# Weights' bound from TensorE products of their upper halves, without identity products, and one more unit with one exponential

## The chip, the cores and the metric

The kernel runs on one core of a Trainium2 chip. The metric is the device time of one execution in microseconds (us). The engines are TensorE (PE in the profile; its weight loads are PEld), VectorE (DVE), ScalarE (ACT), GpSimd (POOL), and SyncE (SP), which issues the transfers. A later kernel is compared with the kernel before by the medians of their runs.

## The reference

A linear attention with random features feeds a two-layer network with GELU. Batch 8, 8 heads, 576 tokens, head size 64, 128 features; the network has model size 512, hidden size 2048, on 8 x 576 = 4608 tokens.

```python
def phi(x):                                  # x: q or k, scaled by D ** -0.25
    proj = np.einsum('bhsd,md->bhsm', x, omega)
    sq = np.sum(x * x, axis=-1, keepdims=True) / 2.0
    h = proj - sq
    h = h - np.max(h, axis=-1, keepdims=True)
    return np.exp(h) / np.sqrt(m)
q_p, k_p = phi(q_s), phi(k_s)
kv = np.einsum('bhsm,bhsd->bhmd', k_p, v)
z = np.sum(k_p, axis=2)
num = np.einsum('bhsm,bhmd->bhsd', q_p, kv)
den = np.einsum('bhsm,bhm->bhs', q_p, z)[..., None] + 1e-06
x = (num / den), heads side by side           # 4608 x 512
h = x @ w_in
g = 0.5 * h * (1.0 + erf(h / sqrt(2)))
out = g @ w_out
```

The two weights come as 64-bit words (the bits of float64) and are made into 32-bit floats on the chip.

## The kernel before, in words

**Attention.** The 64 heads are worked in 32 units of two heads (`units`, four to a batch entry, numbered 0 to 31). Units 0 to 7 are plain, in 32-bit floats (`unit_plain`). A plain unit loads k and q (`load_two`) and v (`load_vraw` with a copy `v_copy` on POOL, or `load_v`), projects both on PE in three steps (`pair`, `shared`, `pair`; lines 657 and 664), takes the maximum of each row on DVE (`top`, line 669), and forms the exponentials of 18 tiles of 128 x 128. In mode 0 (units below `X['m0']`) each tile has an exponential of its own on ACT, with the maximum as bias (`exp_tiles`, line 673). In mode 1 DVE subtracts the maxima in five instructions (`shift_tiles`, line 678) and ACT takes one exponential of the whole unit (`exps`, line 682). Then come k times v on PE (`kv`, line 689), the transposes of q (`q_trans`, `q_copy`, lines 727 and 731), and for each half of the tokens numerator and denominator (`num_plain`, line 737), the reciprocal (`rcp`) and the division (`div`). Units 8 to 31 are split: they work with pairs of high and low parts on all engines.

**Network.** The tokens are cut into 13 blocks: 128 tokens, eleven times 384, then 256. Block 0 is computed with 32-bit products (`mm1` line 1176, `mm2` line 1202) and needs the first 128 tokens, so units 0 to 3. The other blocks use pairs of 16-bit parts, with three products for each (`mm1` line 1181, `mm2` lines 1205 to 1207), and scales that are powers of two.

**Weights.** Each weight comes in eight pieces of 1024 words a partition, w_in first, through two `raw` buffers (`weights_in`). A piece has two transfers of 512 KB (`w_load`), ACT converts the upper words (`w_hi`, line 426) and the lower ones (`w_lo`, line 435), DVE takes the absolute maximum of the raw upper words (`w_rmax`, line 438) and shifts (`w_shift`, line 442), and POOL adds the two (`w_round`, line 453). When the eight maxima of a weight are there, a chain finds the largest of all: `wchain_a` on DVE over the pieces, `wchain_b` a transpose on PE, `wchain_c` on DVE (line 506), `wchain_d` on PE, then the exponent is cut out and the scales are made (`wchain_e`, `wchain_f`). With them each weight is split into two 16-bit parts (`w_high` on ACT, `w_low` on DVE).

**PSUM.** Of the eight banks three go by the name `at`, three by `acc`, two by `h`. The plain units of the first batch entry use all three names for some tiles.

**Order.** Every step is an operation with an engine, a cost and what it reads and writes. They are numbered as they are created. A planner goes through a modelled time and emits for each engine, among the operations that are ready, the one with the earliest due time; due times come from the numbers `STARTS`, `UDUE` and `OFF` and from those in `X`. The operations in `FIRST` are taken in the order of that list, ahead of all others. The order so found is fixed on each engine. Numbers 0 to 5 are constants and omega, 6 to 39 unit 0, 40 to 73 unit 1, 74 to 107 unit 2, 108 to 141 unit 3, 142 to 145 the v of units 4 and 5, 146 to 149 the scale chain of the first batch entry, 151 to 246 the pieces of w_in and then w_out, six operations to a piece, 248 to 253 the scale chain of w_in, 254 to 285 its split. Block 0 has 292 to 373 (292 is its first product), block 1 begins at 421, unit 4 at 582, unit 5 at 614.

**Identity products.** When the planner finds PE free between 5 (`wk0`) and 100 us (`wk`) of its modelled time with nothing to emit, it puts in four products of a 128 x 128 matrix made of bits of the identity (`fill`, line 381), whose result nobody reads. At the very start stand 22 products of zeros (`warm`, line 377).

## Time and profile before

| what | value |
|---|---|
| median of 3 runs | 976.95 us (976.17 to 978.94) |
| the profiled execution | 975.53 us |
| its span, first to last instruction | 973.8 us |
| PE busy | 963.4 us, 99% |
| DVE, ACT, POOL busy | 715.4, 730.0, 350.4 us |
| identity products, line 381 | 312, 21.8 us |

The profile is one execution. A group of instructions reads: line, engine, operation, tile written <- tiles read, shapes, count | busy us, mean ns of one | idle time of its engine just before, and what ended it. A stretch reads: from:to, length, then for each engine busy us and number of instructions, the granted clock of PE, the share of the DMA engines and GB/s. A line of the timeline reads: start us, us, engine, line, operation, tiles, shapes, count [idle time before it <- what ended it]. A line of the waits reads: engine and line <- what it waited for: us in total, times, longest.

### The profile page before, as it was taken

What the parts mean: (1) busy time and instruction counts of PE and PEld (TensorE: products, weight loads), DVE (VectorE), ACT (ScalarE), POOL (GpSimd) and SP (SyncE); (2) the same over time, 40 slices, a digit from 0 to 9 for tenths busy, and PEclk for the clock granted to TensorE, in tenths of its full rate; (3) what the DMA queues carried; (4) which work ended last, traced back from release to release, by engine and by line L of the source; (5) the groups of instructions that cost most, each with busy time, mean ns of one, the idle gap of its engine ahead of it and who ended that gap; (6) DMA issues with size and microseconds to landing.
All of it is one profiled execution on the core that took longest, in us unless ns stands there. A gap on an engine that the chain in (4) does not pass through costs nothing.

```text
span 973.8 us, 18152 instructions
## 1 busy us (share of the span) xinstructions
PE 963.4 (99%) x6324; PEld 602.3 (62%) x6324; DVE 715.4 (73%) x1948; ACT 730.0 (75%) x1504; POOL 350.4 (36%) x560
## 2 busy tenths in 40 slices
PE   8999999999999999999999999999999999999998
PEld 7777665665566666666565665566656656555576
DVE  5899899977888889878797888777767778621111
ACT  6979897887689879787798878877776986643243
POOL 2444334742166264353255335245216522200000
PEclk9999999999999999999999999999999999999999
DMA  8756123321041041031221132022003200000000
GB/s 305 229 182 227 70 73 134 98 82 55 1 118 61 26 139 47 25 91 45 75 82 49 30 127 66 14 72 61 24 33 86 62 23 12 1 33 1 1 34 22
DMA packets 39083, 70.96 MB, mean 73 GB/s; under 512 B 5712, under 2 KB 14288, under 8 KB 38992
## 3 DMA queue, kind: packets, MB, share of 16 engines
q1 hardware_dynamic: 38992, 69.81, 23.1%
q8 instruction: 50, 0.82, 0.4%
q14 instruction: 41, 0.34, 0.1%
HBM read 60.36 MB, written 9.44 MB: 72 GB/s over the span
## 4 chain that ended last, share of the span: by engine, by line
PE 96%; DVE 2%; DMA 1%; ACT 0%; issue 0%; SPq 0%; ACTq 0%; DVEq 0%
PE hb L1181 37%; PE acc L1205 12%; PE acc L1207 12%; PE acc L1206 12%; PE at L746 4%; PE at L924 3%; PE at L902 3%; PE at L1003 2%; PE hb L381 2%; PE hb L1176 2%; PE acc L1202 1%; PE at L657 1%; PE at L737 1%; PE at L689 1%; PE hb L689 1%; PE at L727 1%
## 5 line engine op out<-in xcount | busy, mean ns | idle before, releaser
L1181 PE MATMUL hb<-xh,wih 128*128 128x384 f16 (+1 forms) x768 | 247.2, 322 | 0.6 <-DVE gl L1197 0.4
L1181 PE MATMUL hb<-xl,wih 128*128 128x384 f16 (+1 forms) x768 | 247.2, 322 | 0.0
L1181 PE MATMUL hb<-xh,wil 128*128 128x384 f16 (+1 forms) x768 | 247.1, 322 | 0.0
L894 POOL TENSOR_TENSOR r<-xt,r 64x256 fp32r<-64x256 f32 (+2 forms) x216 | 171.8, 814 | 202.7 <-ACT r L889 161.3
L1205 PE MATMUL acc<-woh,gh 128*128 128x512 f16 (+1 forms) x560 | 211.4, 377 | 0.0
L1207 PE MATMUL acc<-wol,gh 128*128 128x512 f16 (+1 forms) x560 | 210.5, 376 | 0.0
L1206 PE MATMUL acc<-woh,gl 128*128 128x512 f16 (+1 forms) x560 | 210.5, 376 | 0.0
L1197 DVE SCALAR_TENSOR_TENSOR gl<-hb,bs,gh 128x384 f16<-128x384 f32 (+1 forms) x192 | 115.2, 600 | 126.0 <-ACT gh L1193 124.2
L1181 PEld LDWEIGHTS <-wih 128*128 128x128 f16 x1536 | 147.0, 98 | 95.2 <-issue 1.7
L1189 ACT ACTIVATE hb<-hb,bs 128x384 f32<-128x384 f32 (+1 forms) x192 | 104.5, 545 | 86.8 <-PE hb L1181 84.5
L1193 ACT ACTIVATE gh<-hb,bs 128x384 f16<-128x384 f32 (+1 forms) x192 | 109.2, 569 | 51.5 <-PE acc L1207 35.5
L1181 PEld LDWEIGHTS <-wil 128*128 128x128 f16 x768 | 75.1, 98 | 50.2 <-issue 1.6
L889 ACT CAST r<-xt 128x256 fp32r<-128x256 f32 (+2 forms) x216 | 81.5, 403 | 25.8 <-PE at L902 10.5
L1207 PEld LDWEIGHTS <-gh 128*128 128x128 f16 x576 | 56.4, 98 | 64.5
L1205 PEld LDWEIGHTS <-gh 128*128 128x128 f16 x576 | 56.1, 97 | 47.4 <-issue 0.4
L1206 PEld LDWEIGHTS <-gl 128*128 128x128 f16 x576 | 56.5, 98 | 42.1
L803 DVE TENSOR_TENSOR w<-at,rt 64x128 f32<-64x128 f32 (+6 forms) x168 | 54.7, 325 | 4.3 <-DVE rt L770 0.5
L757 ACT ACTIVATE dt<-at,vsc 64x288 f32<-64x288 f32 x96 | 47.6, 495 | 5.2 <-PE at L746 3.0
L902 PE MATMUL at<-om,r 128*128 128x256 f32 x216 | 50.3, 325 | 0.2
L924 PE MATMUL at<-r,om 128*128 128x288 f32 x192 | 50.4, 351 | 0.0
L906 ACT COPY lo<-at 128x256 f32<-128x256 f32 (+1 forms) x120 | 40.4, 349 | 2.2 <-PE at L902 1.5
L963 DVE TENSOR_TENSOR ql<-qt,qh 128x576 fp32r<-128x576 f32 x48 | 37.3, 782 | 6.1 <-ACT qh L960 6.0
(218 smaller groups left out, 1690.6 us busy)
## 6 DMA issues: line engine op xcount, KB each, us to landing
xt<-in_kT SPq DMA_DIRECT2D x56, 288.0 KB, 3.8
xt<-in_qT SPq DMA_DIRECT2D x56, 288.0 KB, 3.6
out_x<-o SPq DMA_DIRECT2D x35, 256.0 KB, 2.1
raw<-in_w_in SPq DMA_DIRECT2D x16, 512.0 KB, 5.2
raw<-in_w_out SPq DMA_DIRECT2D x16, 512.0 KB, 4.6
w<-in_v SPq DMA_DIRECT2D x6, 1280.0 KB, 6.1
wol<-in_v SPq DMA_DIRECT2D x6, 320.0 KB, 5.9
vt<-in_v SPq DMA_DIRECT2D x2, 320.0 KB, 4.1
```

The source lines that it names most:

```text
L803: nc.vector.tensor_tensor(x[r, c0:c1], ps[r, r0:r1], rt[r, r0:r1], op=ALU.mult)
L889: nc.scalar.copy(G['r', u, x][:, 0:b - a], xf[:, a:b])
L894: nc.gpsimd.tensor_tensor(r, xf[D:, a:b], r, op=ALU.subtract)
L902: nc.tensor.matmul(o[:, t], r[:, t * P:(t + 1) * P], om, start=True, stop=True)
L924: nc.tensor.matmul(G['pp', u, NK + g][:, 0:HS], om[:, i], xr_part(u, NK + g), start=(i == 0), stop=(i == 1))
L1181: nc.tensor.matmul(h[:, 0:t], w, (G['xh', n, j], G['xh', n, j], G['xl', n, j])[k][:, 0:t], start=(i == 0), stop=(i == 3 * NJ - 1))
L1189: nc.scalar.activation(h, h, AF.Gelu, scale=G['bs', n][:, 2:3])
L1193: nc.scalar.activation(G['gh', n, c][:, 0:t], G['h', n, c][:, 0:t], AF.Copy, scale=G['bs', n][:, 3:4])
L1197: nc.vector.scalar_tensor_tensor(G['gl', n, c][:, 0:t], G['h', n, c][:, 0:t], G['bs', n][:, 3:4], G['gh', n, c][:, 0:t], op0=ALU.mult, op1 ...
L1205: nc.tensor.matmul(acc, gh[:, s], woh[:, c, c0:c1], start=(c == 0), stop=False)
L1206: nc.tensor.matmul(acc, gl[:, s], woh[:, c, c0:c1], start=False, stop=False)
L1207: nc.tensor.matmul(acc, gh[:, s], wol[:, c, c0:c1], start=False, stop=(c == NF - 1))
```

## The change

- The maximum over the raw upper words (`w_rmax`) is not taken any more. In its place PE multiplies the upper halves (as bf16) of the rounded words with themselves: `w_gram`, eight products of 128 x 128 a piece, summed over four pieces (`GP`) in one PSUM bank. DVE then takes the maximum of that 128 x 128 sum (`w_gmax`). Its diagonal holds sums of squares, so its root bounds the weights; `wchain_e` and `wchain_f` halve the exponent accordingly. A piece still has six operations, with one more for every fourth.
- `wk` goes from 100 to 0: no identity products are put in. (`fill` itself is written a little differently and not called.)
- `m0` goes from 5 to 4: unit 4 takes mode 1 instead of mode 0. `shift_tiles` writes the unit's own tile.
- All numbers of the planner are others, and `FIRST` has 984 entries instead of 752. In it block 0's first product has the number 296, w_in's pieces are 151 to 200, w_out's 201 to 250, the chain of w_in 252 to 257, unit 4 begins at 586, unit 5 at 619.

The diff; of the lists only `FIRST` is shown, up to the entry of block 0's first product:

```diff
--- before.py
+++ after.py
-X = dict(fb=793.51, fbp=-272.45, fb0=327.13, fbb=-89.81, fbw=0.0, pm=0.088, tsw=1.28, wmaxp=0, plain=8, kvp=8, eb0=8, ttr=1,
-         pair=0, amax=0, qm=1, xm=0, km=0, prelu=1, vs=1, rm=1, wk=100.0, wk0=5.0, nd=1, sr=0, pmx=0, m0=5)
...
-FIRST = (1, 3, 0, 2, 6, 7, 8, 40, 4, 5, 42, 110, 76, 144, 41, 142, 10, 9, 151, 157, 44, 13, 43, 11, 14, 15, 47, 74, 16, 45, 17,
-         12, 49, 46, 18, 108, 50, 48, 23, 75, 21, 51, 19, 22, 52, 153, 152, 77, 57, 154, 24, 109, 155, 25, 55, 20, 156, 53,
-         158, 58, 28, 159, 78, 160, 111, 163, 26, 30, 29, 161, 32, 54, 27, 79, 83, 162, 81, 31, 582, 84, 33, 59, 56, 60, 34,
-         61, 85, 169, 112, 80, 35, 164, 165, 62, 66, 166, 167, 36, 63, 168, 115, 67, 82, 37, 113, 171, 170, 86, 114, 175, 38,
-         64, 583, 116, 173, 117, 39, 65, 614, 91, 118, 172, 89, 87, 119, 174, 90, 68, 92, 176, 177, 120, 93, 143, 88, 181, 69,
-         615, 178, 123, 584, 121, 124, 70, 96, 179, 122, 100, 98, 585, 180, 97, 94, 587, 71, 99, 183, 101, 182, 102, 95, 187,
-         72, 588, 125, 185, 586, 73, 184, 103, 130, 145, 589, 131, 126, 134, 186, 132, 647, 104, 135, 127, 133, 590, 128, 105,
-         188, 189, 136, 591, 129, 193, 106, 190, 592, 146, 191, 147, 648, 192, 595, 148, 107, 596, 593, 597, 137, 594, 199,
-         195, 194, 602, 649, 138, 196, 604, 248, 598, 139, 605, 197, 603, 149, 599, 198, 249, 616, 140, 200, 292, 250, 141,
...
+X = dict(fb=647.7, fbp=-229.23, fb0=655.22, fbb=-508.62, fbw=0.0, pm=0.056, tsw=1.28, wmaxp=0, plain=8, kvp=8, eb0=8, ttr=1,
+         pair=0, amax=0, qm=1, xm=0, km=0, prelu=1, vs=1, rm=1, wk=0.0, wk0=5.0, nd=1, sr=0, pmx=0, m0=4, gm=1, rawn=2)
...
+FIRST = (1, 3, 6, 0, 2, 40, 41, 7, 151, 4, 5, 157, 8, 42, 10, 142, 144, 44, 110, 13, 76, 11, 14, 15, 47, 49, 74, 16, 108, 50,
+         45, 12, 17, 152, 18, 158, 154, 75, 9, 21, 46, 19, 43, 23, 48, 160, 51, 20, 57, 24, 22, 77, 153, 28, 58, 111, 78, 159,
+         155, 32, 29, 30, 79, 33, 83, 25, 81, 31, 52, 80, 26, 586, 84, 161, 163, 34, 85, 55, 109, 82, 53, 156, 35, 56, 86, 27,
+         169, 36, 54, 162, 587, 89, 37, 59, 87, 90, 60, 62, 38, 61, 164, 91, 39, 63, 166, 88, 66, 64, 92, 143, 67, 165, 96, 98,
+         97, 167, 100, 65, 101, 99, 112, 170, 68, 115, 171, 176, 113, 117, 172, 116, 168, 619, 118, 173, 69, 114, 119, 70, 588,
+         93, 94, 182, 71, 95, 589, 177, 591, 174, 125, 590, 178, 592, 179, 175, 180, 593, 72, 120, 652, 594, 183, 126, 102,
+         620, 123, 145, 184, 188, 121, 185, 124, 595, 186, 73, 122, 181, 103, 596, 127, 128, 104, 130, 129, 194, 187, 599, 131,
+         134, 132, 653, 597, 189, 105, 600, 598, 133, 135, 191, 190, 136, 146, 106, 601, 192, 147, 107, 137, 195, 607, 201,
+         138, 193, 196, 197, 609, 611, 139, 608, 198, 612, 610, 602, 148, 140, 149, 141, 207, 199, 603, 202, 621, 654, 200,
+         252, 203, 253, 204, 296, 297, 624, 298, 604, 300, 205, 299, 254, 301, 622, 302, 255, 625, 303, 623, 304, 208, 305,
...
@@ -270,6 +281,7 @@
     T0 = [sum(TB[:n]) for n in range(NBLK + 1)]
     assert T0[-1] == NTOK
     NF = F // P
+    GP = 4
     R2 = 2 * S
     NT = R2 // P
     NV = v.shape[3]
@@ -323,7 +335,7 @@
     op = PL.op
     mp, dp, late, G = [], [], [], {}
     bufs = dict(at=3, h=2, acc=3, nm=2, cm=2, ct=2, cg=2, zr=2, km=2, kvz=1, qh=1, kvz2=1, qh2=1, dt=1, rt=1, rc=2, mx=1, nq=1, mc=1, kvs=1,
-                vsc=2, bs=4, be=2, xs=4, raw=2, r=2 if X['xm'] else 3, lo=2, qt=2, ql=2 if X['qm'] else 4, kvh=1, kvl=1, xh=8, xl=8, g=3, gh=3, gl=3, o=2)
+                vsc=2, bs=4, be=2, xs=4, raw=X['rawn'], r=2 if X['xm'] else 3, lo=2, qt=2, ql=2 if X['qm'] else 4, kvh=1, kvl=1, xh=8, xl=8, g=3, gh=3, gl=3, o=2)
     for k, b in bufs.items():
         PL.ring(k, b)
     QW = 2 if X['qm'] else 1
@@ -378,7 +390,7 @@
 
     def fill():
         for i in range(4):
-            nc.tensor.matmul(hb[0][:, T:], iz[:, 0:P], iz[:, P:], start=True, stop=True)
+            nc.tensor.matmul(hb[0][:, T:], iz[:, 0:P], iz[:, P:], start=False, stop=True, skip_group_check=True)
 
     def load_om():
         for r in range(2):
@@ -437,6 +449,15 @@
     def w_rmax(pc):
         nc.vector.tensor_reduce(wmax[:, pc.win, pc.i:pc.i + 1], raw(pc)[2].bitcast(F32), axis=AX.X, op=ALU.max, apply_absolute_value=True)
 
+    def w_gram(pc):
+        o = G['gram', pc.win, pc.i // GP][:, 0:P]
+        for x in range(8):
+            a = pc.b.bitcast(BF16).rearrange("p (x m t) -> p x m t", x=8, t=2)[:, x, :, 1]
+            nc.tensor.matmul(o, a, a, start=(pc.i % GP == 0 and x == 0), stop=(pc.i % GP == GP - 1 and x == 7))
+
+    def w_gmax(win, g):
+        nc.vector.tensor_reduce(wmax[:, win, g:g + 1], G['gram', win, g][:, 0:P], axis=AX.X, op=ALU.max)
+
     def w_shift(pc):
         if X['rm']:
             nc.vector.tensor_scalar(pc.b, pc.b, 3, None, op0=ALU.logical_shift_left)
@@ -494,6 +515,9 @@
         return w32f[:, 0, c], woh[:, c], wol[:, c]
 
     def wchain_a(win):
+        if X['gm']:
+            nc.vector.tensor_reduce(wcm[:, win:win + 1], wmax[:, win, 0:NF // 2 // GP], axis=AX.X, op=ALU.max)
+            return
         w = [i for i in range(NF // 2) if i % 2 == 0 or not X['pmx'] >> (i // 2 + 4 * (1 - win)) & 1]
         st = 2 if len(w) == NF // 4 else 1
         assert st == 2 or len(w) == NF // 2
@@ -509,12 +533,14 @@
         nc.tensor.matmul(G['wps', win][:, P:P + 1], ones, G['wct', win][0:1, 0:1], start=True, stop=True)
 
     def wchain_e(win):
-        nc.vector.tensor_scalar(wsc[:, win, 0:1].bitcast(I32), G['wps', win][:, P:P + 1].bitcast(I32), 0x7ff00000 if X['rm'] else 0x7f800000, None, op0=ALU.bitwise_and)
+        nc.vector.tensor_scalar(wsc[:, win, 0:1].bitcast(I32), G['wps', win][:, P:P + 1].bitcast(I32), 0x7f000000 if X['gm'] else 0x7ff00000 if X['rm'] else 0x7f800000, None, op0=ALU.bitwise_and)
 
     def wchain_f(win):
         e, s, r = (wsc[:, win, i:i + 1].bitcast(I32) for i in range(3))
         one = float(1 << 23)
-        if X['rm']:
+        if X['gm']:
+            nc.gpsimd.tensor_scalar(e, e, 0.5, 65 * one, op0=ALU.mult, op1=ALU.add)
+        elif X['rm']:
             nc.gpsimd.tensor_scalar(e, e, 1.0, -896 * one / 8, op0=ALU.mult, op1=ALU.add)
             nc.gpsimd.tensor_scalar(e, e, 187 * one / 8, 87 * one / 8, op0=ALU.min, op1=ALU.max)
             nc.gpsimd.tensor_scalar(s, e, -8.0, (254 + TOP) * one, op0=ALU.mult, op1=ALU.add)
@@ -544,7 +570,7 @@
         rk, bk = ('raw', win, i), [('w32', win, c) for c in pc.c]
         wl[0] = op('SP', 0.94, w_load, pc, new=[('raw', rk)], size=735e3, after=wl[0])
         op('ACT', 1.08, w_hi, pc, r=[rk], w=bk if X['rm'] else [rk + ('hi',)])
-        if X['rm']:
+        if X['rm'] and not X['gm']:
             op('DVE', 1.23, w_rmax, pc, r=[rk], w=[('wmax', win, i)])
         op('ACT', 1.08, w_lo, pc, r=[rk], w=pc.lk if pc.l is not None else [rk + ('lo',)])
         if not X['sr']:
@@ -559,6 +585,12 @@
         op('POOL', 2.4 + 0.4 * X['sr'], w_round, pc, r=[rk, rk + ('lo',)] + (pc.lk if pc.l is not None else []), w=bk)
         if X['sr'] and not X['prelu']:
             op('DVE', 1.21, w_sign, pc, r=[rk], w=bk)
+        if X['gm']:
+            g = ('gram', win, i // GP)
+            op('PE', 0.46, w_gram, pc, r=bk, w=[g] if i % GP else [], new=[] if i % GP else [(ANY[:2], g)])
+            if i % GP == GP - 1:
+                op('DVE', 0.25, w_gmax, win, i // GP, r=[g], w=[('wmax', win, i // GP)])
+            return
         if X['rm']:
             return
         if X['pmx'] >> (i // 2 + 4 * (1 - win)) & 1:
@@ -675,7 +707,7 @@
     def shift_tiles(u, k, ts):
         n = len(range(2 * NT)[ts])
         pv = G[k][:, 0:n * P].rearrange("p (t m) -> p t m", m=M)
-        nc.vector.tensor_tensor(et[:, ts], pv, G['nm', u][:, ts].unsqueeze(2).broadcast_to([P, n, M]), op=ALU.add)
+        nc.vector.tensor_tensor(u.et[:, ts], pv, G['nm', u][:, ts].unsqueeze(2).broadcast_to([P, n, M]), op=ALU.add)
 
     def exps(*us):
         for u in us:
```

More of the change, by code (lines that the diff above doesn't have):

```diff
@@ L26 @@
 TBS = (128,) + (384,) * 11 + (256,)
-X = dict(fb=793.51, fbp=-272.45, fb0=327.13, fbb=-89.81, fbw=0.0, pm=0.088, tsw=1.28, wmaxp=0, plain=8, kvp=8, eb0=8, ttr=1,
-         pair=0, amax=0, qm=1, xm=0, km=0, prelu=1, vs=1, rm=1, wk=100.0, wk0=5.0, nd=1, sr=0, pmx=0, m0=5)
-STARTS = (526.64, 413.1, 498.14, -519.29, 750.73, 290.96, 409.8, 1471.02, 410.3, 561.38, 1804.53, 1092.9, 2449.47, 1437.07)
-UDUE = (138.05, 1052.37, 451.76, -315.56, -8.29, -412.87, -648.85, -667.31, -702.59, -616.51, 659.91, -322.47, 26.1, 555.78,
[4 rows of a table removed]
@@ L51 @@
-FIRST = (1, 3, 0, 2, 6, 7, 8, 40, 4, 5, 42, 110, 76, 144, 41, 142, 10, 9, 151, 157, 44, 13, 43, 11, 14, 15, 47, 74, 16, 45, 17,
[31 rows of a table removed]
+X = dict(fb=647.7, fbp=-229.23, fb0=655.22, fbb=-508.62, fbw=0.0, pm=0.056, tsw=1.28, wmaxp=0, plain=8, kvp=8, eb0=8, ttr=1,
+         pair=0, amax=0, qm=1, xm=0, km=0, prelu=1, vs=1, rm=1, wk=0.0, wk0=5.0, nd=1, sr=0, pmx=0, m0=4, gm=1, rawn=2)
+STARTS = (412.42, 653.5, 441.15, -677.42, 743.14, 400.93, 780.18, 825.26, 441.66, 285.14, 1439.49, 1000.86, 1810.77, 1167.1)
@@ new lines @@
+UDUE = (176.77, 1015.59, 463.19, -234.55, 109.96, -452.15, -855.33, -883.87, -808.78, -588.47, 512.64, -629.9, -195.61, 817.08,
[4 rows of a table added]
+OFF = dict(block_be=0.84, block_high=-2.56, block_low=0.9, block_out=-1.79, block_spread=10.38, bound_a=162.44, bound_b=14.89,
+           chain_a=64.97, chain_b=-25.49, chain_c=7.47, chain_d=-64.81, den=-73.77, div=132.1, exp_tiles=-0.29, exps=-29.94,
+           g_high=9.53, gelu=17.68, k_low=35.67, k_shift=0.47, kv=10.92, kv_a=0.51, kv_b=42.42, kv_b2=3.03, kv_c=48.29,
+           kv_d=3.07, kv_split=31.59, kvz_plain=-6.79, load_dup=26.25, load_om=-6.31, load_two=-7.52, load_v=29.83,
+           load_vraw=-33.05, load_vst=-4.66, mm1=-64.6, mm2=-18.41, nothing=111.04, num=-106.7, num_plain=-95.35, p2=-3.6,
+           pair=-18.86, proj=26.72, proj_add=13.93, proj_lo=0.73, proj_q=40.57, q_back=23.41, q_blocks=-0.43, q_copy=10.83,
+           q_high=62.65, q_low=-58.16, q_max=50.95, q_max2=25.79, q_max3=3.98, q_max4=-14.62, q_max5=44.93, q_max6=2.41,
+           q_shift=125.5, q_trans=13.48, scale_om=0.18, shared=-33.97, shift_tiles=33.5, split_om=-1.75, store=-0.29,
+           store_dma=97.81, top=1.3, v_a=62.18, v_b=-12.99, v_copy=-2.44, v_max=127.3, v_scales=-6.73, v_spread=11.66,
+           w_gmax=-126.84, w_gram=38.4, w_hi=-0.45, w_high=9.25, w_lo=-0.61, w_low=0.47, w_shift=26.8, warm=2.44,
+           wchain_a=-0.4, wchain_b=3.35, wchain_c=15.67, wchain_e=-21.18, wchain_f=-4.54, x_high=20.23, x_low=-8.93,
+           zeros=-15.48)
```

12 lines of the change are left out of this document (removed), and 64 rows, old and new, of tables (FIRST, UDUE).

## The prediction

> **What bounds the kernel now.** The page comes first: the share of each engine, the slices, and the chain that ended last.
>
> ```profile
> span 973.8 us, 18152 instructions
> ...
> PE 963.4 (99%) x6324; PEld 602.3 (62%) x6324; DVE 715.4 (73%) x1948; ACT 730.0 (75%) x1504; POOL 350.4 (36%) x560
> ...
> DVE  5899899977888889878797888777767778621111
> ACT  6979897887689879787798878877776986643243
> ...
> PE 96%; DVE 2%; DMA 1%; ACT 0%; issue 0%; SPq 0%; ACTq 0%; DVEq 0%
> ```
>
> TensorE (PE) is busy for 99% of the span and owns the chain; VectorE (DVE) and ScalarE (ACT) come to nine tenths only in the first slices. So the time is: when useful work on PE becomes dense, plus all that PE has left to do from there. A busy PE need not be a useful one, since the identity products count too. The second view is therefore the busy time by stretches, of all instructions and then of the identity products (line 381) and of the start-up products (line 377) alone.
>
> ```profile
> core 0: us, PE busy (x) PEld busy (x) DVE busy (x) ACT busy (x) POOL busy (x), PEclk, DMA share, GB/s
> 0.00:10.00 10.00, 6.99 (x62) 5.34 (x64) 2.75 (x14) 2.42 (x5) 1.94 (x8) 1.00 0.68 229
> 10.00:30.00 20.00, 18.90 (x244) 16.40 (x240) 12.62 (x28) 16.82 (x49) 7.06 (x7) 1.00 0.96 316
> 30.00:65.00 35.00, 34.48 (x396) 27.80 (x395) 31.53 (x80) 30.84 (x78) 15.50 (x10) 1.00 0.71 222
> 65.00:112.00 47.00, 45.98 (x364) 34.85 (x364) 43.31 (x86) 40.99 (x61) 19.64 (x20) 1.00 0.49 169
> 112.00:157.00 45.00, 45.00 (x286) 26.17 (x285) 41.59 (x108) 37.45 (x77) 19.08 (x29) 1.00 0.24 64
> 157.00:200.00 43.00, 42.91 (x262) 26.08 (x261) 38.60 (x113) 34.82 (x72) 22.52 (x35) 1.00 0.35 113
> ```
>
> ```profile
> 0.00:10.00 10.00, 0.40 (x4) 0.23 (x4) 1.00 0.68 229
> 10.00:30.00 20.00, 6.75 (x100) 5.84 (x100) 1.00 0.96 316
> 30.00:65.00 35.00, 10.59 (x152) 9.21 (x152) 1.00 0.71 222
> 65.00:112.00 47.00, 4.06 (x56) 3.60 (x56) 1.00 0.49 169
> ```
>
> ```profile
> 0.00:10.00 10.00, 4.23 (x22) 2.93 (x22) 1.00 0.68 229
> ```
>
> Before 65 us PE is busy for 60.4 us, but 17.7 of these are identity products and 4.2 start-up products: 38.4 us are useful. From 65 to 112 us only 4.06 are identity products and 1.02 idle; from 112 us on nothing is spare. The first product of block 0 (line 1176) starts at 64.8 us:
>
> ```profile
> L1176 PE MATMUL hb<-xa,w x128: 272/275/377, 64.8 to 107.9; 128*128 128x128 f32 x128
> ```
>
> So there are two stages. Up to 65 us units 0 to 3 go through DVE and ACT (31.5 and 30.8 of the 35 us from 30 to 65), and PE waits for them. From 65 us on PE sets the end. What the change is worth is the lead L by which block 0 starts earlier, plus what leaves PE's own queue after that, less what is put there.
>
> **The change, part by part.**
>
> *Maxima out, and what the order puts ahead of block 0.* The rows that price it (line 438 is the maximum over raw weights, 682 the one exponential of a unit; the last row is the sum of line 673, the exponentials of single tiles, over the first 200 us):
>
> ```profile
> L438 DVE TENSOR_REDUCE wmax<-raw 128x1 f32<-128x1024 f32 x16 | 19.3, 1207 | 1.0 <-DMA raw<-in_w_in 1.0
> L678 DVE TENSOR_TENSOR et<-at,nm 128x512 f32<-128x512 f32 (+1 forms) x10 | 5.9, 622 | 0.0
> L442 DVE TENSOR_SCALAR w<-w 128x1024 int32<-128x1024 int32 x16 | 10.8, 677 | 0.0
> L506 DVE TENSOR_REDUCE ct<-at 1x1 f32<-1x128 f32 x2 | 0.5, 254 | 0.0
> L435 ACT ACTIVATE w<-raw 128x1024 int32<-128x1024 uint32 x12 | 14.2, 1185 | 0.0
> L731 ACT COPY qh<-at 128x512 f32<-128x512 f32 (+1 forms) x11 | 5.4, 518 | 0.0
> L682 ACT ACTIVATE et<-et x16: 2122/2124/2129, 81.6 to 826.3; 128x2304 f32<-128x2304 f32 x16
> ```
>
> ```profile
> sum 200.00, ACT 26.54; mean ACT 4.42
> ```
>
> Five units of 18 tiles make 90, so a tile's exponential is 0.295 us. In the order written out by hand, block 0's first product is number 292 at place 230 of the old list and 296 at place 238 of the new one. I count what stands ahead of it in each. On DVE eight maxima go (8 x 1.207 = 9.7 us); two small maxima over PSUM come (0.25 each, by the 128-element reduce of line 506), five shift instructions of unit 4 (5.9 / 10 x 5 = 2.95), one weight shift (0.68) and one division (taken as a shift's 0.59): DVE is 4.9 us lighter. On ACT unit 4's 18 tiles go (5.3); one exponential (2.12), one weight conversion (1.19) and one copy (0.49) come: 1.5 us lighter. Over the whole kernel DVE gets 19.3 - 1.0 - 2.95 = 15.3 us lighter and ACT 3.2; but after 65 us both run beside a full PE, and what they save there buys nothing.
>
> L is 1.5 us if ACT sets the stage and 4.9 if DVE does. From 30 to 65 us they are busy for 30.84 and 31.53 us, too close to choose, so I take the middle: L = 3.2 us.
>
> *Identity products out.* Before 65 us they stand where PE waits anyway: 0. After 65 us they and the idle time make 4.06 + 1.02 = 5.1 us that useful work can take: -5.1. New idle time there is taken as 0, because the next stretch, which has no identity product, shows 45.00 busy of 45.00; were it not so, as much of the 5.1 would stay idle, so the other end is 0.
>
> *Products of the weights in.* Each of 16 pieces brings eight products of 128 columns. The nearest row is 52 identity products, of that type and shape, in one run:
>
> ```profile
> 8.66 0.37 PE L657 MATMUL at<-om,xt 64*128 64x128 f32 x1 [1.96 <-DMA xt<-in_kT]
> ...
> 10.34 3.08 PE L381 MATMUL hb<-ident 128*128 128x128 bf16 x52
> ```
>
> That is 59 ns each and 0.47 us a piece. Eight pieces lie ahead of block 0, in PE's idle time; eight after it, on the path: +3.8 us. They read every second half word, so the far end is the 4-byte product of line 1176, at most its 275 ns each, +17.6; pipelined as those are, I take 3.8, from the same type and shape. One of the six PSUM banks that the units use is held through four pieces. What DVE waited for the units' products from 10 to 112 us could grow:
>
> ```profile
> DVE nm L669 <- PE acc L664: 3.0, 2, 2.6
> DVE nm L669 <- PE acc L657: 2.2, 1, 2.2
> ```
>
> Doubled, that is 5.2 us; I take 0, since five banks are left, and let the no-change rival hold it.
>
> *The chain to the weights' scale* grows: a piece's bound used to need its raw words alone, and now conversion, shift and rounding too. In PE's queue the last product of the first weight (place 228) and the chain's transpose (236) stand ahead of block 0. What they wait for (ACT, DVE, POOL):
>
> ```profile
> 60.79 1.18 ACT L435 ACTIVATE w<-raw 128x1024 int32<-128x1024 uint32 x1
> 62.15 0.69 DVE L442 TENSOR_SCALAR w<-w 128x1024 int32<-128x1024 int32 x1
> 62.98 2.37 POOL L453 TENSOR_TENSOR w<-w 128x1024 int32<-128x1024 int32 x1 [3.81 <-ACT qh L731]
> ```
>
> That rounding ends at 65.35; with 0.47 of products and two small maxima of 0.25 the transpose could go at about 66.4, 1.6 us behind today's start of block 0. With the engines 1.5 to 4.9 us lighter it goes at 61.5 to 64.9. So it takes nothing in the forecast, and all of L where the stage does not shorten.
>
> *Loads.* SP now issues two weight pieces, four transfers, ahead of the first v.
>
> ```profile
> raw<-in_w_in SPq DMA_DIRECT2D x16, 512.0 KB, 5.2
> ```
>
> From 10 to 30 us the DMA share is 0.96, so 2.1 MB at 316 GB/s hold v back by up to 6.6 us, while ACT, idle for 3.2 us there, gets its weights sooner. Ends -3.2 and +6.6; I take 0, since only PE needs v, and DVE and ACT have the weights meanwhile.
>
> *The later blocks* get other due times. From 112 to 200 us PE idles 0.09 us, so nothing is to be won, and the same work keeps it full: 0.
>
> **Sum.** The profiled execution took 975.53 us, 1.7 over its span. 975.53 - 3.2 - 5.1 + 3.8 = 971.0. It lies 1.4 under the median of 976.95 (976.17 to 978.94), so the forecast for the median is 972.4. About 0.3%, 2.9 us, is what a measurement of this kernel can tell from no change.
>
> **Where a rule speaks against the change.** These are products of 256 columns, the first of the trace and those of the last block:
>
> ```profile
> L377 PE MATMUL hb<-w 128*128 128x256 bf16 x22 | 4.2, 380 | 1.1 <-DVE w L368 1.1
> L1181 PE MATMUL hb<-xh,wil 128*128 128x256 f16 x64 | 17.4, 272 | 0.0
> ```
>
> The first take 380 ns, the later ones 272, though the granted clock reads 1.00 for both: PE starts slow, and that column doesn't show it. Without identity products the 3.08 us at 10.34 become idle, and more after them. The longest pause of today, 1.96 us ahead of 8.66, did not bring the slow state back for the products that follow it. The Trainium skill, "TensorE: Matmul & The Clock Gate", section "What's actually happening", says that an idle window of about 3.4 us puts the clock back to half. No run so far shows a pause as long; by that rule the slow rival below decides.
>
> **The rivals.**
>
> *Slower: PE runs slow before block 0.* From 10 to 65 us its useful work is 53.4 - 17.3 = 36.0 us, with eight pieces' products 39.8, in 55 us. Every us of that work at half speed adds one; beyond 15.2 us of it PE itself holds block 0 back. With six tenths slow (23.9) it is 8.7 over, and L is -8.7 instead of +3.2: 984.3 for the median. For it: 17.3 us of that stretch are kept busy by identity products alone. Against it: the pause of 2 us did nothing, and the new products fill some pauses. Chance 0.13, with 0.04 more for gaps that new due times open in later blocks.
>
> *No change: the longer chain holds block 0.* If the lighter engines do not bring the last rounding forward, block 0 starts 1.6 us late and the other terms give 1.3 back: 975.8, 977.2 for the median. For it: POOL waited 3.81 us ahead of that rounding, for ACT's stream, which gets little lighter. Against it: the shift ahead of it is DVE's, which does. Chance 0.20.
>
> *Faster: the stage closes up.* ACT idles 7.3 us from 10 to 65 us, partly behind DVE. If a lighter DVE and earlier weights let it run full, L is 7.3 + 1.5 = 8.8: 965.4, and 966.8 for the median. PE's 39.8 us still fit. Against it: both engines wait for loads and for PE's results there as well. Chance 0.17.
>
> **How the numbers follow.** The forecast has the other 0.46, with a range of its own from 970 (L = 4.9) to 976 (products at about twice their price). The fast rival and most of the forecast lie under 974.0: faster 0.60. The no-change rival and the rest of the forecast: 0.23. Slower, beyond 979.9: 0.17. The range of 8 in 10 runs from 964, below the fast rival, to 981, which leaves out most of the slow one.
>
> **What the next profile would show.** L: line 1176's first start, at 61.6 instead of 64.8 if I am right, at 56.0, 66.4 or 73.5 by the rivals. No row of line 381. The new products at 0.47 us a piece, and a PE without idle time in the stretch that replaces 65 to 112; idle time there would mean that identity products hid a wait for DVE or ACT. A slow PE shows in the units' products as in 380 against 272 ns. DVE's total should fall by about 15 us, ACT's by 3. If the time moves while block 0's start doesn't, my reading in two stages is wrong.

## The result, and the profile after

The changed kernel takes 993.75 us (median; 993.27 to 995.35) against 976.98 for the kernel before (976.17 to 978.94): a ratio of 1.0168, 95% interval [1.0153, 1.0184]. I forecast 972.4 with 964 to 981, so the time lies outside the range, on the other side. The profiled execution took 993.55 us, 1.8 over its span. Two of the runs below have one execution each far off the rest (1010.79 us of b_gram_hb_tt, 2580.51 of b_noeps), which their rows in the table leave out.

The page of the changed kernel, the lines that answer to those of before:

```profile
span 991.8 us, 17683 instructions
...
PE 965.6 (97%) x6140; PEld 599.9 (60%) x6140; DVE 719.6 (73%) x1941; ACT 725.1 (73%) x1487; POOL 349.3 (35%) x560
...
PEclk7989999999999999999999999999999999999999
...
PE 82%; DVE 9%; ACT 3%; DMA 3%; issue 1%; POOL 1%; SPq 1%; ACTq 0%; POOLq 0%
```

PE's busy time is that of before (963.4), though the identity products are gone; its share of the chain fell from 96% to 82%, and DVE's rose from 2% to 9%. The first slice and the third show a granted clock below full, which before had not. Then the same stretches as before:

```profile
core 0: us, PE busy (x) PEld busy (x) DVE busy (x) ACT busy (x) POOL busy (x), PEclk, DMA share, GB/s
0.00:10.00 10.00, 8.49 (x82) 6.47 (x84) 4.62 (x17) 3.97 (x11) 0.70 (x6) 1.00 0.75 230
10.00:30.00 20.00, 14.78 (x95) 13.33 (x93) 5.90 (x14) 11.93 (x33) 7.95 (x7) 0.66 0.56 200
30.00:65.00 35.00, 29.46 (x263) 21.75 (x259) 29.46 (x70) 24.80 (x62) 11.94 (x10) 0.90 0.74 237
65.00:112.00 47.00, 44.50 (x371) 33.69 (x371) 41.09 (x86) 42.29 (x60) 25.46 (x21) 1.00 0.63 208
112.00:157.00 45.00, 44.34 (x302) 28.15 (x300) 38.12 (x94) 36.82 (x71) 11.69 (x17) 1.00 0.20 53
```

From 10 to 30 us DVE is busy for 5.90 us instead of 12.62, and from 30 to 65 us ACT for 24.80 instead of 30.84: both engines that I took for the limit of this stage now stand idle in it. Block 0 starts late:

```profile
L1208 PE MATMUL hb<-xa,w x128: 273/275/378, 74.2 to 125.1; 128*128 128x128 f32 x128
```

It starts at 74.2 us instead of 64.8, where I forecast 61.6. That is 9.4 of the 18.0 us between the two spans (973.8 and 991.8). The rest comes after it, as stretches from block 0's start to block 1's first store, to block 2's, to block 5's and to the end show, first of the kernel before, then of the changed one:

```profile
64.78:203.16 138.38, 137.27 (x937) 89.21 (x936) 126.01 (x309) 116.54 (x215) 61.47 (x84) 1.00 0.36 114
203.16:272.31 69.15, 69.15 (x417) 41.02 (x415) 55.77 (x152) 53.68 (x115) 20.81 (x46) 1.00 0.15 48
272.31:495.22 222.91, 222.91 (x1372) 135.92 (x1371) 185.49 (x547) 184.69 (x390) 105.61 (x171) 1.00 0.24 71
495.22:973.75 478.53, 473.92 (x2913) 286.85 (x2911) 301.41 (x824) 325.19 (x659) 138.19 (x236) 1.00 0.14 41
```

```profile
74.20:212.53 138.33, 135.28 (x915) 87.43 (x915) 122.72 (x297) 112.61 (x209) 59.09 (x82) 1.00 0.36 110
212.53:284.75 72.22, 72.22 (x447) 43.05 (x444) 57.56 (x154) 56.10 (x116) 19.86 (x47) 1.00 0.15 47
284.75:512.87 228.12, 226.30 (x1388) 137.24 (x1387) 187.06 (x549) 185.97 (x393) 106.43 (x173) 1.00 0.24 70
512.87:991.70 478.83, 472.30 (x2898) 285.03 (x2896) 304.02 (x820) 321.31 (x656) 138.71 (x236) 1.00 0.14 41
```

The first stretch is as long as before, the second 3.1 us longer, the third 5.2, the last 0.3. In the second PE is busy throughout and has 30 products more: work that used to lie ahead of block 1's stores. In the third PE idles 1.8 us.

What stands ahead of block 0 in the changed kernel, from the timeline (start, duration, engine, line, operation):

```profile
50.95 2.36 POOL L474 TENSOR_TENSOR w<-w 128x1024 int32<-128x1024 int32 x1 [2.86 <-PE hb L721]
51.43 1.91 DVE L796 TENSOR_SCALAR rc<-rt 128x9 f32<-128x9 f32 x1
...
64.52 0.17 DVE L796 TENSOR_SCALAR rc<-rt 128x9 f32<-128x9 f32 x1
64.73 2.12 ACT L714 ACTIVATE et<-et 128x2304 f32<-128x2304 f32 x1
...
69.38 2.36 POOL L474 TENSOR_TENSOR w<-w 128x1024 int32<-128x1024 int32 x1 [2.10 <-DVE w L463]
69.62 2.28 PE L721 MATMUL at<-vt,et 128*128 128x65 f32 x18
70.28 1.49 DVE L796 TENSOR_SCALAR rc<-rt 128x9 f32<-128x9 f32 x1
...
71.80 0.63 PE L456 MATMUL acc<-w 128*128 128x128 bf16 x8
73.49 0.27 DVE L459 TENSOR_REDUCE wmax<-acc 128x1 f32<-128x128 f32 x1
74.10 0.27 PE L527 MATMUL at<-ident,wcm 128*1 128x128 f32 x1 [0.57 <-DVE wcm L519]
74.20 1.05 PE L1208 MATMUL hb<-xa,w 128*128 128x128 f32 x8
```

Three things are to be seen. The last rounding on POOL that block 0 needs ends at 71.74 (65.35 before), its products follow at 71.80, the small maximum at 73.49, the chain's transpose at 74.10, block 0 at 74.20: the bound is now the end of the weights' whole path. Unit 4's one exponential (64.73 to 66.85) stands ahead of its keys times v (69.62). And DVE's addition of a constant to 9 denominators (line 796) takes 0.17 us where POOL is idle and 1.49 to 1.91 beside a rounding, and ends when the rounding does. Three of these additions stand in the chain that ended at block 0 (start, us):

```profile
44.48 1.77 DVE rc L796
...
51.43 1.92 DVE rc L796
...
70.28 1.50 DVE rc L796
```

In the first 112 us:

```profile
L764 DVE TENSOR_SCALAR rc<-rt 128x9 f32<-128x9 f32 x12 | 4.2, 353 | 0.4
```

```profile
L796 DVE TENSOR_SCALAR rc<-rt 128x9 f32<-128x9 f32 x11 | 10.9, 990 | 0.4
```

The first row is of the kernel before, the second of the changed one: one addition less, 6.7 us more.

### The profile page after: what moved, and what is told of

It is laid out like the page before. It is cut to its first block, busy times and chain, and to the rows that moved or that the text cites. A ratio compares the mean times of both kernels' runs of the same rounds, so it can differ in the third digit from the quotient of the medians.

```text
span 991.8 us, 17683 instructions
## 1 busy us (share of the span) xinstructions
PE 965.6 (97%) x6140; PEld 599.9 (60%) x6140; DVE 719.6 (73%) x1941; ACT 725.1 (73%) x1487; POOL 349.3 (35%) x560
## 4 chain that ended last, share of the span: by engine, by line
PE 82%; DVE 9%; ACT 3%; DMA 3%; issue 1%; POOL 1%; SPq 1%; ACTq 0%; POOLq 0%
PE hb L1213 34%; PE acc L1237 11%; PE acc L1238 11%; PE acc L1239 11%; PE at L778 3%; PE at L934 2%; PE at L1035 2%; PE at L956 2%; DMA wol<-in_v 1%; PE hb L1208 1%; DVE rc L796 1%; DVE mx L961 1%; PE acc L1234 1%; PE hb L721 1%; DVE gl L1229 1%
## 5 line engine op out<-in xcount | busy, mean ns | idle before, releaser
L926 POOL TENSOR_TENSOR r<-xt,r 64x256 fp32r<-64x256 f32 (+2 forms) x216 | 167.4, 791 | 234.5 <-ACT r L921 161.8
L934 PE MATMUL at<-om,r 128*128 128x256 f32 x216 | 53.6, 339 | 1.4 <-POOL r L926 1.3
L956 PE MATMUL at<-r,om 128*128 128x288 f32 x192 | 48.4, 346 | 0.9 <-POOL r L926 0.6
L364 POOL TENSOR_SCALAR w<-et 128x256 f16<-128x256 f32 (+1 forms) x65 | 24.9, 411 | 60.7 <-ACT et L714 57.9
```

The lines of the kernel that those rows point to most:

```text
L926: nc.gpsimd.tensor_tensor(r, xf[D:, a:b], r, op=ALU.subtract)
L934: nc.tensor.matmul(o[:, t], r[:, t * P:(t + 1) * P], om, start=True, stop=True)
L956: nc.tensor.matmul(G['pp', u, NK + g][:, 0:HS], om[:, i], xr_part(u, NK + g), start=(i == 0), stop=(i == 1))
```

## The experiments

Two kinds of kernel were run. Some keep the changed kernel's order of instructions on every engine and undo one thing (names with a_); others keep the old order and put in one thing (b_). "Block 0" is its first product in one profiled execution; between executions with the same order ahead of it it moved by up to 2.2 us (74.2 and 75.8 in `after` and `a_lateb`, 77.6 and 75.4 in `a_sp` and `a_sp_lateb`). It moved by 3.1 between b_gram_hb and b_gram_hb_tt, whose additions took as long (5.5 us by 112 us in both). So differences of 3 us and less there are not read, and larger ones are held against the medians. The profiled executions of b_nofill and b_m04 lie at the long end of their ten (979.4 and 987.8 us, medians 977.0 and 982.2), so where block 0 stands in them is late for these kernels too. The ratios are to the kernel before, in the same job.

| run | block 0, us | median, us | ratio, 95% interval |
|---|---|---|---|
| before / after | 64.8 / 74.2 | 976.98 / 993.75 | 1.0168 [1.0153, 1.0184] |
| a_fill | 75.6 | 994.52 | 1.0179 [1.0143, 1.0215] |
| a_v | 73.9 | 992.68 | 1.0155 [1.0135, 1.0174] |
| a_sp | 77.6 | 994.48 | 1.0177 [1.0160, 1.0194] |
| a_nogram | 78.2 | 996.45 | 1.0187 [1.0168, 1.0206] |
| a_exp4 | 74.4 | 992.78 | 1.0162 [1.0140, 1.0185] |
| a_noeps | 70.2 | 987.86 | 1.0107 [1.0092, 1.0123] |
| a_tt | 76.8 | 993.00 | 1.0160 [1.0137, 1.0182] |
| a_lateb | 75.8 | 990.16 | 1.0138 [1.0119, 1.0157] |
| a_sp_lateb | 75.4 | 991.15 | 1.0146 [1.0131, 1.0161] |
| b_nofill | 67.1 | 977.03 | 0.9993 [0.9974, 1.0012] |
| b_nomax | 63.5 | 975.00 | 0.9977 [0.9959, 0.9996] |
| b_gram | 76.0 | 989.57 | 1.0129 [1.0108, 1.0150] |
| b_gram_free | 75.8 | 987.65 | 1.0093 [1.0066, 1.0121] |
| b_gram_hb | 70.0 | 987.76 | 1.0110 [1.0084, 1.0137] |
| b_gram_hb_tt | 66.9 | 985.57 | 1.0084 [1.0061, 1.0107] |
| b_m04 | 77.9 | 982.24 | 1.0064 [1.0040, 1.0087] |
| b_latea | 64.6 | 980.82 | 1.0041 [1.0026, 1.0056] |
| b_noeps | 65.1 | 975.52 | 0.9990 [0.9977, 1.0002] |

**First theories: the clock, the first loads, the later order.**

a_fill, identity products put back at PE's three pauses ahead of block 0:

```diff
+(22 x fill)  kv u0
+(12 x fill)  products of weight piece 4
+( 8 x fill)  q_trans u4
```

> The changed kernel, every engine's order as it is, with 42 groups of four identity products put back into PE's queue where PE stood for over 2 us (22 ahead of unit 0's kv, 12 ahead of the fifth weight piece's products, 8 ahead of unit 4's transposes). Clock theory (the missing identity products let PE fall to half speed, and that makes block 0 late): granted clock 1.00 throughout, first product of block 0 at about 67 instead of 74.2 us, 986 to 988 us. Load theory (unit 0's v lands late behind the weight pieces, and the slow clock only fills time that is lost anyway): block 0 at 72 to 74, 992 to 994 us.

a_v, the order of SP's queue:

```diff
 load_two u0, load_om, load_two u1
+load_vraw u0, load_vraw u1
 w_load in0, w_load in1
-load_vraw u0, load_vraw u1
```

> The changed kernel, with the loads of units 0's and 1's v issued ahead of the first two weight pieces instead of behind them; nothing else moved. Load theory: unit 0's kv starts at about 11 instead of 15.7 us, the pause of 5.2 us shrinks under 2 us, the clock does not fall at 14.7, block 0 starts at 66 to 69, 985 to 989 us. Clock theory, if the pauses are due to the missing products alone: the clock falls all the same a little later, block 0 at 72 or more, 991 to 994 us.

b_nofill, the old order on every engine:

```diff
-(78 x fill)
```

> The kernel before, every engine's order as it is, with its 78 groups of identity products left out and nothing in their place. Clock theory: PE falls to half speed at least once before 65 us (the 3 us pause at 10.3 becomes idle), block 0 starts 4 to 9 us later, 981 to 986 us. Rival (identity products are of no use where v comes early): no fall, block 0 at 64 to 65, and 2 to 4 us less after it: 973 to 977 us.

a_lateb, from the end of block 1 on:

```diff
-every engine's work in the changed kernel's order
+every engine's work in the old order
```

> The changed kernel up to the end of block 1 (its last store), and from there on all operations in the order of the kernel before. Plan theory (the new due times cost the later blocks about 8.5 us, by PE's waits for VectorE): 984 to 987 us, the stretch from block 1's last stores to the end at about 771 instead of 779 us. Rival (the later blocks lose what the late start and the units' lag behind it leave them): 992 to 995 us.

The granted clock did fall in the changed kernel, and in b_nofill, to half:

```profile
14.70:28.30 13.60, 12.58 (x65) 11.69 (x67) 3.43 (x9) 8.56 (x25) 6.85 (x6) 0.50 0.43 160
55.60:62.40 6.80, 5.71 (x41) 5.19 (x41) 6.59 (x17) 3.15 (x12) 2.54 (x2) 0.50 0.60 189
```

```profile
9.80:30.30 20.50, 19.45 (x121) 17.10 (x117) 10.66 (x20) 12.32 (x34) 6.34 (x6) 0.50 0.78 264
71.30:74.70 3.40, 3.24 (x17) 1.56 (x17) 3.25 (x8) 0.80 (x3) 2.93 (x7) 0.50 0.37 87
```

The first two rows are of the changed kernel, the others of b_nofill. That is 20.4 us at half speed in the one and 23.9 in the other. Yet putting the identity products back (mean clock 0.996 instead of 0.989) did not make the changed kernel faster, though about 7 us at half speed were left of the 20.4 (from 20 us on), and b_nofill is as fast as the kernel before. So the clock is not the cause of most of the 16.8 us. It is not free either: in two of b_nofill's ten executions the mean clock stayed at 0.998, with spans of 969.5 and 970.5, where those at 0.987 have 976.9 to 977.6 and the kernel before had a median span of 975.5 in that job. In these two executions the old order without identity products is 5.5 us ahead of the kernel before; in the others it loses that again. Early v started the first unit's keys times v at 10.9 us instead of 15.7, and gained 1.1 us in the median. The later order gave back 3.6 us, so a_lateb lies between my two ranges.

**Second theories: SP's queue, and the products themselves.**

a_sp, the order of SP's queue (a key load that waits for a buffer stood ahead of a weight piece):

```diff
-load_two u4 0, w_load in2, load_two u3 1, w_load in3
+load_two u3 1, w_load in2, load_two u4 0, w_load in3
-load_two u6 0, load_two u5 1, w_load in6
+w_load in6, load_two u5 1, load_two u6 0
```

> The changed kernel, with the order of SP's queue alone changed: weight pieces 2 and 6 are issued ahead of the key loads of units 4 and 5 that stand in front of them in the changed order. Those loads wait for a buffer that unit 2 or 3 frees, and piece 2 went out at 28.95 us instead of 19.70, piece 6 at 53.18 instead of 43.00. Queue theory (the blocked queue makes block 0 late): piece 2 goes out by 20 us, block 0 starts at 66 to 70 us instead of 74.2, and the time is 986 to 990. Order theory (what ACT, DVE and PE do ahead of block 0 comes in an order that is longer by itself, and the pieces land early for nothing): block 0 stays at 73 or later and the time at 992 to 995.

a_sp_lateb is a_sp with the later order of a_lateb.

> As the run before, and from the end of block 1 on every engine's work in the old order. By that later order alone the changed kernel came to 990.2. Queue theory: both gains add up, 982 to 986. Order theory: 989 to 992, as with the later order alone.

b_gram, the old order without identity products:

```diff
-w_rmax (16 x DVE)
+w_gram (16 x 8 products on PE, each piece's behind its w_round), w_gmax (4 x DVE)
+other PSUM banks for some of the units' tiles, as one bank is held
```

> The old order without its identity products (977.0 by itself, block 0 at 67.05 us), with the products of the weights in place of the maxima: each piece's products stand in PE's queue behind that piece's rounding, nothing else is planned anew. Plan theory (the parts of the change are harmless, its new order is what costs): 974 to 979, block 0 at 64 to 68. My own first sum (a lighter DVE brings block 0 forward): block 0 3 to 5 us earlier, 972 to 975 with the eight pieces' products on the path. Chain theory (the bound now waits for the last piece's rounding, and a PSUM bank is held): block 0 at 69 or later, 981 or more.

b_latea, from the end of block 1 on (its first part keeps the identity products, so it is to be compared with the kernel before itself):

```diff
-every engine's work in the old order
+every engine's work in the changed kernel's order
```

> The old kernel without identity products to the end of block 1, then every engine's work in the order of the changed kernel; maxima and the old exponentials stay. Plan theory (the changed order of the later units makes PE wait or work more): 981 to 985.5, with the 8.5 us between block 1's stores and the end that the changed kernel shows, or at least 4 of them. Rival (the later loss is only what a late start leaves behind): 976 to 978.5.

The queue theory failed for what the run could test: piece 6 was issued at 50.75 instead of 53.18 us and nothing came of it. Piece 2 was not issued earlier but at 30.89, since unit 3's query load, which I had put ahead of it too, was not issued before 30.47; so that a free queue for piece 2 gains nothing isn't shown. a_sp_lateb came to 991.15, as a_lateb (990.16). The later order costs 3.6 us by itself (980.82 against 977.24 in the job), as it gave back 3.6 in the changed kernel. And the products in place of the maxima cost 12.5 us on the old order, which neither my sum nor the plan theory allowed.

**Third: which part costs what.**

b_nomax, b_nofill with a maximum over 8 words:

```diff
-nc.vector.tensor_reduce(wmax[...], raw(pc)[2].bitcast(F32), ...)
+nc.vector.tensor_reduce(wmax[...], raw(pc)[2][:, 0:8].bitcast(F32), ...)
```

> The old order without identity products (977.0 by itself, block 0 at 67.05 us); each weight maximum reads 8 words instead of 1024, so eight times about 1.05 us of DVE go ahead of block 0 and as many after it, and nothing comes in. The bound is that of those few words. First term of my sum (a lighter DVE brings block 0 forward by up to its own saving): block 0 at 62 to 65, time 972 to 975. Rival (DVE is not what sets the stage; ACT and the waits between the engines do): block 0 at 66 to 67, time 976 to 977.5.

b_gram_free, b_gram with products of the identity:

```diff
-nc.tensor.matmul(o, a, a, ...)
+nc.tensor.matmul(o, iz[:, 0:P], iz[:, 0:P], ...)
```

> The old order with the weights' products in place of the maxima (989.6, block 0 at 76.0 us), in the same order on every engine and with the same PSUM banks, but the products are of the identity, which is there from the start; so no product waits for a rounding. The bound is a constant. Chain theory (products at the head of PE's queue wait for POOL's rounding, and the units' work behind them waits too): block 0 at 66 to 69, 976 to 980. Bank theory (the PSUM bank that is held, and the other banks that the units take for it, cost the time): block 0 at 74 to 76, 987 to 990.

a_nogram:

```diff
-for x in range(8): nc.tensor.matmul(o, a, a, ...)
-w_gmax: tensor_reduce(wmax[...], G['gram', win, g][:, 0:P], ...)
+w_gmax: tensor_reduce(wmax[...], ident, ...)
```

> The changed kernel in its own order without the weights' products: PE has none of their work, waits or banks, and the bound is a constant that DVE reduces from the identity. Chain theory: block 0 at 66 to 70 instead of 74.2, time 981 to 987 (7.5 us of products go as well). Order theory (the order of the other engines, fixed with the products in mind, is as late without them): block 0 at 72 or later, 985 to 991.

a_noeps:

```diff
-nc.vector.tensor_scalar(rc, rv[:, :, 0], EPS, None, op0=ALU.add)
-nc.vector.reciprocal(rc, rc)
+nc.vector.reciprocal(rc, rv[:, :, 0])
```

> The changed kernel in its own order without the 9-element addition of a small constant to the denominators of units 0 to 7 (the reciprocal reads its operand directly). In the changed kernel that addition took 1.77, 1.92 and 1.50 us on the chain ahead of block 0, each ending with POOL's rounding, and 0.17 us where POOL is idle. Port theory (DVE's addition waits while POOL rounds, and that is on the path): block 0 at 69 to 71.5, time 988 to 991. Rival (what waits behind it waits for something else anyway): block 0 at 73 or later, 992 to 994.

b_nomax is the first term of my sum by itself: block 0 came 3.6 us earlier (67.05 to 63.48), where I had said 3.2 between 1.5 and 4.9. But this is not shown to be the maxima's doing: the two executions also differ in the granted clock (0.987 and 0.992 in the mean), the medians differ by 2.0 with intervals that overlap, and at a like clock (0.990 and 0.991) four executions of b_nofill took 975.9 to 977.2 us and seven of b_nomax 973.2 to 980.0. b_gram_free speaks against waits as the only cause: its products need no rounding, and block 0 stayed at 75.8. a_nogram went the wrong way, outside both of my ranges: without the products the clock stood at a mean of 0.89 in the stretch from 65 to 112 us, and block 0 came 4 us later. a_noeps is the one thing undone ahead of block 0 that moved the changed kernel much: block 0 4.0 us earlier, the time 5.9 lower (986.7 to 989.3, against 993.3 to 995.4).

**Last: the bank, the exponential, the form of DVE's addition.**

b_gram_hb, b_gram with the sums in the spare columns of the two hidden-layer banks (the bound that comes out there is not the weights' own):

```diff
-o = G['gram', pc.win, pc.i // GP][:, 0:P]
+o = hb[1 - pc.win][:, T:]
-other PSUM banks for some of the units' tiles
+the banks of the old order
```

> The old order without identity products, with the weights' products in place of the maxima as before (989.6 with a PSUM bank held, 987.7 with nothing to wait for), but the products now add up in the last 128 columns of the two hidden-layer banks, which the units don't use: no bank is held and the units keep the banks of the old order. Bank theory (holding one of six banks over four pieces is what makes block 0 late): block 0 at 63.5 to 67, time 974 to 979. Rival (the products' place in PE's queue and the longer chain cost it): block 0 at 70 or later, 983 or more.

b_m04, b_nofill with:

```diff
-exp_tiles u4 (ACT, 18 tiles)
+shift_tiles u4 (DVE), and behind the last: exps u4 (ACT)
```

> The old order without identity products (977.0, block 0 at 67.05 us), with one change: unit 4 takes one exponential over all its 18 tiles behind its last shift, and its shifts stand on DVE where its exponentials stood on ACT; maxima stay. By my sums DVE gets 2.95 us more ahead of block 0 and ACT 3.2 less. Harmless: block 0 at 66 to 69, 976 to 979. If unit 4's weighted keys are what block 0 waits for (PE's queue has them ahead of it), the exponential comes later by up to 2 to 5 us: block 0 at 69 to 72, 979 to 983.

a_tt:

```diff
-nc.vector.tensor_scalar(rc, rv[:, :, 0], EPS, None, op0=ALU.add)
+nc.vector.tensor_tensor(rc, rv[:, :, 0], epst, op=ALU.add)
```

> The changed kernel in its own order; the 9-element addition to the denominators is a two-operand addition with a constant tile instead of one with an immediate number, so nothing is left out. It tells whether the wait for POOL hangs on the form of DVE's instruction. Port theory in this form (an instruction with one operand from memory and an immediate waits for POOL's rounding, one with two operands doesn't): 0.1 to 0.3 us each, block 0 at 70 to 71, 987 to 990, as without the addition (987.9). Rival (any such DVE instruction waits): still up to 2 us each beside a rounding, block 0 at 73 to 75, 992 to 995.

b_gram_hb_tt has both edits.

> Products in the spare columns and the two-operand addition, in the old order without identity products. If both theories hold: block 0 at 62 to 65 and 971 to 976, below the old kernel. If only that of the bank holds: as with the spare columns alone.

a_exp4 is the changed kernel with b_m04's edit reversed, and b_noeps the old kernel with the edit of a_noeps.

> The changed kernel in its own order with its third part undone: unit 4 gets its exponentials tile by tile on ACT again, each at the place where its shift stood, and neither shifts on DVE nor the one exponential over 18 tiles. By that part alone block 0 came 10.8 us later on the old order. Exponential theory (unit 4's weighted keys wait for the one exponential behind the last shift, and PE's queue has them ahead of block 0): block 0 at 66 to 70.5 instead of 74.2, time 984 to 990. Order theory (the new order was made around it, and its other waits end as late): block 0 at 73 or later, 991 to 994.

> The old kernel, with its identity products, without the 9-element addition of a small constant to the denominators of units 0 to 7. Twelve of them took 4.2 us in the first 112 us, up to 1.9 us each beside a rounding on POOL. Port theory carried over: block 0 1 to 2.5 us earlier (62.3 to 63.8), time 973.5 to 976. Rival (on the old order they lie beside other waits): block 0 within 0.5 us of 64.8, 976.5 to 977.5.

With no bank held, and the units back in the banks of the old order, block 0 comes 6.0 us earlier (76.0 to 70.0). Part of that can be the clock, which no run holds still: PE ran 23.9 us at half speed ahead of block 0 in b_gram's execution and 17.1 in this one. What is left over b_nomax's 63.5 goes with the weights' path. From b_gram_hb's timeline:

```profile
64.99 2.35 POOL L677 TENSOR_TENSOR w<-w 128x1024 int32<-128x1024 int32 x1 [3.19 <-ACT w L650]
...
67.39 0.63 PE L659 MATMUL hb<-w 128*128 128x128 bf16 x8 [2.66 <-POOL w L677]
68.69 0.27 PE L730 MATMUL at<-ident,wcm 128*1 128x128 f32 x1 [0.67 <-DVE wcm L722]
69.98 0.94 PE L1411 MATMUL hb<-xa,w 128*128 128x128 f32 x6
```

PE idles 2.66 us in front of the last piece's products until the rounding has ended at 67.34; b_nomax's transpose went at 61.14, before that rounding (61.46 to 63.81) had begun, since it needed the raw words alone. So each holds block 0 back by itself: the bank without the wait to 75.8 (b_gram_free), the wait without the bank to 70.0. b_gram_hb's time did not follow (987.8 against b_gram's 989.6): its execution is 2.1 us longer than b_nofill's from block 0 to block 1's first store and 2.3 from there on. That loss isn't explained; the out weights' sums stand in banks that the network uses then.

The exponential, from b_m04's timeline:

```profile
66.28 2.12 ACT L917 ACTIVATE et<-et 128x2304 f32<-128x2304 f32 x1 [3.63 <-DVE et L913]
68.55 4.19 PE L924 MATMUL at<-vt,et 128*128 128x65 f32 x18 [7.59 <-ACT et L917]
...
77.85 0.94 PE L1411 MATMUL hb<-xa,w 128*128 128x128 f32 x6
```

```profile
63.00:76.70 13.70, 8.15 (x35) 6.37 (x35) 6.06 (x18) 6.31 (x8) 3.54 (x2) 0.50 0.40 127
```

PE waits 7.59 us for it, and then does unit 4's keys times v in 4.19 us instead of 2.28 (line 721 of the changed kernel, above), while the granted clock stands at 0.50. So block 0 is 10.8 us later than in b_nofill's execution; the median is 5.2 higher, and at a like mean clock (0.990 to 0.992) five executions took 980.0 to 982.2 us, about 4 more than b_nofill's. But a_exp4, which takes it back out of the changed kernel, moves nothing (992.8): there PE's queue has the weights' last pieces and unit 3 ahead of the same place, and they end as late.

The addition, in a_tt and then in a_noeps (minimum, median and maximum in ns):

```profile
L1001 DVE TENSOR_TENSOR rc<-rt,epst x16: 170/186/1923, 32.0 to 167.1; 128x9 f32<-128x9 f32 x16
```

```profile
L999 DVE RECIPROCAL rc<-rt x16: 216/216/218, 32.3 to 159.8; 128x9 f32<-128x9 f32 x16
```

With a second operand from memory it waits as before, so the port theory in my form (only the immediate waits) is wrong; the reciprocal never waits, though seven of the twelve by 112 us start inside a rounding. The Trainium skill, "SBUF — State Buffer", section "Who interferes with whom", says that DVE and GpSimd share one pair of ports as an exclusive lock, which a DVE instruction takes in a two-port mode (one that a `tensor_scalar` can enter) or with two operands in SBUF; the traces agree for both forms. b_gram_hb_tt therefore says nothing of a faster addition: its additions are as long as b_gram_hb's, and why its block 0 came 3.1 us earlier stays open. Leaving the addition out of the old kernel gains nothing that can be told (0.9990 [0.9977, 1.0002]); the longest there was 1.24 us, and not up to 1.9 as I had put it. No run is a version that beats both kernels and leaves nothing out.

## Why the prediction was wrong, step by step

**"Maxima out, and what the order puts ahead of block 0": L = 3.2.** This is the step that failed; it measured -9.4. Its count was right for what goes: DVE's own instructions are 15.0 us lighter as I summed (maxima 19.3 out; 1.1 and 3.2 in for small maxima and shifts). What that is worth by itself is not shown: b_nomax's 3.6 at block 0 can be the clock. The step failed for what comes. I counted the one exponential as 18 tiles of ACT saved; it makes unit 4's keys times v, ahead of block 0 in PE's queue, wait for all its tiles, and alone costs the old order 10.8 us at block 0 in the one execution, 5.2 in the median. I let the products lie "in PE's idle time" at no cost; in b_gram block 0 stands 9.0 us behind b_nofill (both ran 23.9 us at half speed) and 12.5 behind b_nomax, and 6.0 less with no bank held, which I had bounded at 5.2 and taken as 0. And I took durations as fixed: DVE's total did not fall by 15 us but rose from 715.4 to 719.6, so the rest of its work took 19 us longer; the additions are 6.7 of that by 112 us, and without them block 0 came 4.0 earlier (a_noeps). No run prices the other 12.

These prices do not add up to 9.4, for the new order is made around them. In the changed kernel's own order the addition's wait is about 4.0 of the 9.4 us. That the additions hold block 0 back there is shown by the chain, by a_noeps and by its time; the size rests on two executions, of which a_noeps's also ran less at half speed (13.7 us against 20.4). The other 5.4 are not tied to one part: undoing the exponential, the products, v's place or the clock one at a time did not bring them back (a_nogram, without the products, ran 27 us at half speed, so it is no clean test of them), so what is left is the order as a whole, with all engines idle in turn. That is argued, not shown.

**"The chain to the weights' scale grows."** Right mechanism, wrong size. I had the transpose at 61.5 to 64.9, about 1 us behind the last rounding, taking nothing. That rounding ended at 71.74, and the transpose came 2.36 us behind it, since the small maximum stood behind a division and two copies in DVE's queue. Of the three rivals the no-change one had this mechanism; it lacked that the roundings themselves could come later. The slow rival came nearest by its numbers (block 0 at 73.5 and 984.3 us), but by luck: the slow products ahead of block 0 that it counted on were not what held block 0 back in a_fill.

**Identity products, -5.1.** Near in the two executions of b_nofill in which the clock holds (5.5), which may be chance, since no trace shows where block 0 stood in them; 0 in the median. In the changed kernel the stretch from block 0 to block 1's first store is as long as before (138.33 against 138.38 us), with PE idle for 3.05 us instead of 1.11, so of -5.1 and +3.8 together nothing shows there. The slow rival's mechanism is there, but the path ahead of block 0 was rarely PE's: 20 us at half speed cost the changed kernel nothing that a_fill could win back. The granted clock stood at half behind PE's pauses of 7.59 us in b_m04 and 5.22 in the changed kernel, but shorter pauses were followed by it too: in the changed kernel it reads half from 55.6 us on, 1.9 us into a pause of 2.95, and in b_nofill from 9.8 on, 0.6 us behind a pause of 1.95. The pause of 1.96 in the kernel before was not followed by it. The rule that I weighed (the Trainium skill, "TensorE: Matmul & The Clock Gate", section "What's actually happening": an idle window of about 3.4 us puts the clock back to half) fits the two long pauses only; read as a length that one pause must reach, it does not hold here, and the pause of 2 us that I held against the slow rival proved nothing.

**Products of the weights, +3.8.** The price of one is right: eight take 0.63 us with the last one's 0.22, so 59 ns apart. That the eight pieces behind block 0 cost 3.8 on the path, no run shows.

**Loads, 0.** Right within 1.1 us, as far as v's place alone goes (a_v).

**Later blocks, 0.** Wrong by 8.5 in the profiles. Of this 3.6 us are the changed order of the later units, shown from both sides (a_lateb, b_latea). The 3.1 us of block 2's stretch are work that the changed order leaves behind block 1's stores: b_gram, b_m04 and the others that start block 0 at 76 to 78 in the old order have 69.2 there, and a_lateb still has 72.9. The other 1.8 are not explained. I argued from a stretch in which PE idles 0.09 us that nothing could be won there, and forgot that it could be lost.
